# A delta-rule and feed-forward kernel: the first pair of chunks with another order, other queues and fewer norm steps

## Chip, cores and metric

One core of one Trainium2 chip. The metric is the device time of one execution in microseconds (us). The engines are PE (TensorE's products; PEld is its weight load), VectorE (DVE), ScalarE (ACT), GpSimd (POOL) and SyncE (SP). Transfers are issued by the queues of SP, ACT and POOL.

## The reference, cut to what matters

```python
# q, k, v: (4, 8, 768, 48), beta: (4, 8, 768), w_in: (384, 2048), w_out: (2048, 384)
k_n = k / (np.linalg.norm(k, axis=-1, keepdims=True) + 1e-06)
for t in range(S):
    y[:, :, t] = np.einsum('bhd,bhde->bhe', q[:, :, t], state)
    v_old = np.einsum('bhde,bhd->bhe', state, kt)
    state = state + bt[:, :, :, None] * np.einsum('bhd,bhe->bhde', kt, vt - v_old)
x = y.transpose(0, 2, 1, 3).reshape(B * S, H * D)
h = x @ w_in
g = np.where(h >= 1, h, np.where(h <= -1, 0.0, (h + 1) ** 2 / 4))
return g @ w_out
```

A recurrence over 768 steps for each of 32 heads, and behind it two matrix products with a clipped square between them, in float32. The two weight matrices come as 64-bit floats and are converted on the chip.

## The kernel before

The 768 steps are cut into 12 chunks of 64, and two chunks make a pair, so there are six pairs. For a chunk, the recurrence is turned into products: a gram matrix of the keys (gram_k, L229) and of keys and queries (gram_q, L242), the inverse of a unit triangular matrix for each head, and a chain of four products with the running state: chain_r, chain_u, chain_y, chain_d (L434 to L571). The inverse is made in three steps. Its diagonal blocks of 16 are solved on VectorE for a pair at once, with the 128 lanes as heads and blocks (lanes, L289; solve, L333: 15 steps of two operations; unlanes, L366, which scales the result and transposes it back into the tile XT). PE then merges blocks of 16 into 32 (merge16_a, merge16_b) and of 32 into 64 (merge32), each with a copy on ScalarE or VectorE behind it. In lanes, norms (L267) makes the norms of the keys from the diagonal of the gram matrix: a root on ScalarE and a step that sharpens it on VectorE.

The feed-forward part works on a pair's 512 token columns, for 16 tiles of 128 hidden units: up (L670) is nine products into one tile h, three operations of ScalarE and one of VectorE make s, a cast on ScalarE (ghi, L790) and a subtraction on VectorE (glo, L791) split it into a high and a low part, and down (L679) adds 12 products to the output's sums. For the first pair the first six tiles are run for the first chunk alone and later again for the second, so that this part can start as soon as chunk 0 is done.

Each weight tile f is 768 KB and is unpacked in five steps: grow (ScalarE, L187), shift and join (VectorE, L193 and L199), cast (ScalarE, L203), low (VectorE, L206). Up for tile f needs all five.

Every engine runs its list in order. The order around the first pair is written by hand. K, Q, KV and weight loads are issued at the start by load_k, load_q, load_kv and weight_loads; then PE runs the grams, 25 filling products on zeros (L629, two passes each in the trace), the merges and the chain of chunk 0. Between a stage's products and the copies that empty them, the letters of FRONT are run, and in the items of the feed-forward part those of FILL: A and D are the next weight step on ScalarE and VectorE, w and W the next weight load through SP or ACT, l the next other load, L a piece of lanes for the second pair of chunks, s, t, v and z half of scaling the values of chunk 0 to 3, m and M a mask of the queries, S a solve step, U a piece of unlanes, B a copy back. PIECES says in which half item PE runs which stage of chunks 1 to 3. The queues of the loads reuse eight semaphores in turn, so a load waits for the eighth before it.

At the end store_last (L703) copies the four output tiles and sends each in two halves.

## Time and profile before

| what | value |
|---|---|
| runs shown | median 610.14 us, 609.32 to 612.75 (3 runs) |
| the profiled execution | 611.8 us, of which the span of the core's instructions is 610.1 |
| mean granted clock of PE | 0.948 of full speed |
| busy share of the span | PE 95%, PEld 83%, DVE 65%, ACT 64%, POOL 5% |
| bytes moved | 42.77 MB, mean 70 GB/s |
| weight transfers | 16 of 768 KB, 14 from SP and 2 from ACT, median 5.7 and 5.4 us to landing |

The page cuts the span into 40 slices of 15.25 us and gives the busy share of each in tenths. A table of stretches gives the same for windows that one chooses. A timeline gives each instruction's start and duration, how long its engine stood idle before it, and what ended that. Busy time of PE is modelled from its pipelined products, so a full PE need not be at its peak; the granted clock says at what share of full speed it ran.

### The profile page before, as it was taken

The page shows a single profiled execution, that of the slowest core. Times are in us where ns is not written, and L with a number is a line of the kernel's source. Part 1 is how long each engine was busy: PE and PEld are TensorE (multiplying, and loading weights), DVE is VectorE, ACT ScalarE, POOL GpSimd, SP SyncE. Part 2 cuts the span into 40 slices and gives each one's busy share as a digit, 9 for nine tenths or more (in the row PEclk, how much of TensorE's full clock was granted, in tenths as well). Part 3 has the DMA queues.
Part 4 walks back from the last instruction along what each step waited for, and adds up shares of the span by engine and source line. Part 5 has one row for each costly group of instructions (what it writes and reads, how often), then busy time and mean ns, then how long its engine had stood idle before and what let it go on. Part 6 is the DMA issues. An engine that isn't in the chain of part 4 may idle for free.

```text
span 610.1 us, 21744 instructions
## 1 busy us (share of the span) xinstructions
PE 577.8 (95%) x9576; PEld 506.4 (83%) x9576; DVE 395.8 (65%) x835; ACT 393.2 (64%) x683; POOL 31.9 (5%) x63
## 2 busy tenths in 40 slices
PE   8847989799989999999999999999999999999996
PEld 7747978688978888888888888888888888889986
DVE  4977789982488963489954489954589944333332
ACT  3537688559756578646587647586746586666663
POOL 6110000010020000020000020000020000000000
PEclk8557599989999999999999999999999999999999
DMA  5672727210224110225110225111134000020001
GB/s 142 200 273 87 288 59 227 75 33 3 65 74 126 37 31 12 62 55 128 46 31 16 60 64 132 31 31 36 38 88 111 1 2 17 10 57 1 0 1 52
DMA packets 32542, 42.77 MB, mean 70 GB/s; under 512 B 7056, under 2 KB 27152, under 8 KB 32448
## 3 DMA queue, kind: packets, MB, share of 16 engines
q1 hardware_dynamic: 31072, 38.94, 22.1%
q10 hardware_dynamic: 1120, 2.36, 1.2%
q8 instruction: 75, 1.23, 0.9%
q14 instruction: 19, 0.16, 0.1%
q0 software_dynamic: 256, 0.08, 0.1%
HBM read 34.47 MB, written 4.72 MB: 64 GB/s over the span
## 4 chain that ended last, share of the span: by engine, by line
PE 68%; ACT 10%; SPq 6%; DVE 6%; DMA 6%; issue 2%; DVEq 0%; ACTq 0%
PE h L675 27%; PE o L690 27%; DMA wt<-in_w_dram 3%; PE ch L481 3%; ACT GG L429 2%; ACT s L795 2%; ACT XT L431 2%; PE ch L439 2%; PE ch L248 2%; PE ch L455 1%; PE ch L417 1%; PE ch L554 1%; PE ch L419 1%; ACT s L827 1%; DMA Q<-in_kqb_dram 1%
## 5 line engine op out<-in xcount | busy, mean ns | idle before, releaser
L675 PE MATMUL h<-xb,wt 128*128 128x512 f32 (+1 forms) x918 | 228.6, 393 | 4.6 <-DMA xb<-wt 2.3
L690 PE MATMUL o<-wt,ghi 128*128 128x384 f32 x768 | 200.7, 343 | 0.0
L675 PEld LDWEIGHTS h<-xb,wt 128*128 128x128 f32 x918 | 165.5, 193 | 38.8 <-issue 2.4
L829 DVE TENSOR_TENSOR s<-h,s 128x512 f32<-128x512 f32 (+1 forms) x102 | 66.7, 654 | 120.3 <-ACT s L827 120.0
L690 PEld LDWEIGHTS o<-wt,ghi 128*128 128x128 f32 x768 | 137.7, 189 | 7.1
L690 PE MATMUL o<-wt,glo 128*128 128x384 f32 x384 | 130.0, 339 | 1.9 <-DVE glo L791 1.9
L790 ACT CAST ghi<-s 128x512 fp32r<-128x512 f32 (+1 forms) x102 | 60.8, 596 | 102.0 <-DVE s L829 93.1
L795 ACT ACTIVATE s<-h,half 128x512 f32<-128x512 f32 (+1 forms) x102 | 67.6, 663 | 38.9 <-PE h L675 38.1
L791 DVE TENSOR_TENSOR glo<-s,ghi 128x512 fp32r<-128x512 f32 (+1 forms) x102 | 66.6, 653 | 38.7 <-ACT ghi L790 38.7
L690 PEld LDWEIGHTS o<-wt,glo 128*128 128x128 f32 x384 | 72.4, 189 | 2.8 <-DVE glo L791 2.8
L795 ACT ACTIVATE s<-s,one 128x512 f32<-128x512 f32 (+1 forms) x102 | 71.7, 702 | 2.3
L827 ACT ACTIVATE s<-s 128x512 f32<-128x512 f32 (+1 forms) x102 | 61.9, 607 | 3.2
L350 DVE TENSOR_TENSOR pr<-A 128x30 f32<-128x30 f32 (+14 forms) x120 | 39.3, 328 | 6.4 <-POOL A L321 4.5
L352 DVE TENSOR_TENSOR A<-A,pr 128x30 f32<-128x30 f32 (+14 forms) x120 | 39.9, 332 | 4.4
L481 PEld LDWEIGHTS ch<-Q,SU 64*64 64x64 f32 (+3 forms) x1056 | 22.5, 135 | 4.5 <-ACT ghi L790 1.5
L481 PE MATMUL ch<-Q,SU 64*64 64x64 f32 (+3 forms) x1056 | 24.7, 222 | 0.7 <-ACT SU L464 0.7
L262 DVE TENSOR_TENSOR Q<-ch,mask 64x512 f32<-64x512 f32 (+1 forms) x30 | 20.6, 687 | 0.9 <-PE ch L248 0.4
L321 POOL TENSOR_SCALAR_AFFINE_SELECT A<-A 128x1024 f32<-128x1024 f32 x4 | 5.1, 1265 | 301.3 <-DMA xb<-X 257.1
L187 ACT ACTIVATE xb<-wt 128x768 f32<-128x768 f32 x16 | 14.5, 905 | 8.9 <-DMA KV<-in_kv_dram 4.7
L417 PEld LDWEIGHTS ch<-XT,GG 32*32 32x32 f32 x768 | 14.9, 113 | 6.3 <-issue 4.2
L417 PE MATMUL ch<-XT,GG 32*32 32x32 f32 x768 | 16.4, 200 | 2.7 <-issue 1.0
L429 ACT ACTIVATE GG<-ch 32x512 f32<-32x512 f32 x24 | 14.1, 589 | 6.5 <-PE ch L417 6.2
(151 smaller groups left out, 595.1 us busy)
## 6 DMA issues: line engine op xcount, KB each, us to landing
wt<-in_w_dram SPq DMA_DIRECT2D x14, 768.0 KB, 5.7
out_dram<-wx SPq DMA_DIRECT2D x44, 96.0 KB, 2.2
KV<-in_kv_dram SPq DMA_DIRECT2D x36, 96.0 KB, 2.4
KV<-in_kv_dram SPq DMA_DIRECT2D x72, 48.0 KB, 2.3
KV<-in_kv_dram SPq DMA_DIRECT2D x12, 192.0 KB, 2.7
xb<-X SPq DMA_DIRECT2D x60, 32.0 KB, 2.0
K<-in_kqb_dram SPq DMA_DIRECT2D x12, 128.0 KB, 2.7
Q<-in_kqb_dram SPq DMA_DIRECT2D x12, 128.0 KB, 2.7
```

The costliest lines, as they stand in the source:

```text
L350: nc.vector.tensor_tensor(out=pr, in0=A[:, 0:n, j:j + 1].broadcast_to([P, n, m]), in1=A[:, j:j + 1, j + 1:32].broadcast_to([P, n, m]), op= ...
L352: nc.vector.tensor_tensor(out=A[:, 0:n, j + 1:32], in0=A[:, 0:n, j + 1:32], in1=pr, op=ALU.add)
L417: nc.tensor.matmul(y1[r:r + 32, u], GG[r + 32:r + 64, ga, u, 0:32], XT[r + 32:r + 64, ga, u, 32:64], start=True, stop=True)
L429: nc.scalar.mul(out=GG[r:r + 32, ga, :, 0:32], in_=y1[r:r + 32], mul=-1.0)
L481: nc.tensor.matmul(yy[i][o * C:o * C + C, e, p], SF[rows, u:u + C], w_[rows, x, k, :], **how)
L675: nc.tensor.matmul(h[:, cols(bs)], WT[f][:, 0, x, k * P:(k + 1) * P], XB[G][:, y, k, cols(bs)], start=(n == 0), stop=(n == 8))
L690: nc.tensor.matmul(oacc[G, k], (ghi, glo)[x][:, k * P:(k + 1) * P], WT[f][:, 1, y, :], start=(new and n == 0), stop=(left[G, b] == 0 and n ...
L790: nc.scalar.copy(out=ghi[:, c], in_=s[:, c])
L791: nc.vector.tensor_tensor(out=glo[:, c], in0=s[:, c], in1=ghi[:, c], op=ALU.subtract)
L795: nc.scalar.activation(out=out, in_=in_, func=AF.Relu, bias=bias, scale=scale)
L827: nc.scalar.activation(out=s[:, c], in_=s[:, c], func=AF.Square)
L829: nc.vector.tensor_tensor(out=s[:, c], in0=h[:, c], in1=s[:, c], op=ALU.max)
```

## The change

In the first lines of the program:
- load_k(1) issues four of its six loads from POOL instead of ACT;
- weight tiles 2, 3 and 4 are issued by SP ahead of load_kv(1), instead of tiles 2 and 3 behind it; ACT no longer issues weights;
- nine warm-up products of PE instead of 14.

In the first pair's work:
- norms reads the diagonal of the gram matrix in place, adds 1e-30 inside the root by a bias, and writes where the result is needed: one copy and one maximum on VectorE go;
- the copies of chunk 1 in lanes(0) are made in halves, four instead of two;
- the transpose of the norms is placed later;
- unlanes scales and transposes half s = 1 first, then half s = 0, instead of both at once;
- FRONT, FILL and PIECES have other values.

In store_last the copies of tiles 2 and 3 change engines, and each tile's second half is sent by ACT, POOL, POOL and ACT, where ACT sent all four.

```diff
-WARM = 14
+WARM = 9
 FRONT = (
-    "AL,L", ",WA", "sL,Amm", "DDmsD,", ",WAADw", "t,", "AtDDD,A")
+    "wsAALLsL,", "D,", "DD,", ",mm", "mt,AtA", "Dw,", "DADA,")
 FILL = (
-    "DD,,D,,w,AA", "ADA,D,D,DA,,B", ...
+    ",D,D,,,DAD", "ADD,Dw,ABADA,,DM,wlA", ...
-PIECES = ((0, "a1"), (1, "r1"), (2, "b1"), (4, "c1"), ... (8, "y1"), (11, "d1"), (16, "q2"), ...
+PIECES = ((1, "a1 r1"), (3, "b1"), (4, "c1"), ... (8, "y1"), (10, "d1"), (17, "q2"), ...
...
-    load_k(1, (nc.sync, nc.scalar))
+    load_k(1, (nc.sync, nc.gpsimd))
...
     load_kv(0)
+    weight_loads(2, 5)
     load_kv(1)
-    weight_loads(2, 4)
...
-    def norms(n):
-        y = sb.tile([P, 32], F32, name="y0")[:, 0:n.shape[1]]
-        r = sb.tile([P, 32], F32, name="r1")[:, 0:n.shape[1]]
-        nc.scalar.activation(out=y, in_=n, func=AF.Sqrt)
-        nc.vector.tensor_scalar(out=r, in0=y, scalar1=1e-30, scalar2=None, op0=ALU.max)
-        nc.vector.reciprocal(out=r, in_=r)
+    def norms(n, out):
+        y = sb.tile([P, 32], F32, name="y0")
+        r = sb.tile([P, 32], F32, name="r1")
+        nc.scalar.activation(out=y, in_=n, func=AF.Sqrt, bias=tiny)
+        nc.vector.reciprocal(out=r, in_=y)
...
-            for r in (0, C):
-                (nc.scalar.copy if G else nc.vector.tensor_copy)(out=x[r:r + 32, :, 32:64], in_=x[r:r + 32, :, 0:32])
+            for u in (half(0), half(1)) if (G, g) == (0, 1) else (slice(0, NU),):
+                for r in (0, C):
+                    (nc.scalar.copy if G else nc.vector.tensor_copy)(out=x[r:r + 32, u, 32:64], in_=x[r:r + 32, u, 0:32])
...
-        nc.vector.tensor_copy(out=n, in_=A.rearrange("l j t -> l (j t)")[:, 0:1024:33])
-        r = norms(n)
-        N = S["N", G] = sb.tile([P, 32], F32, name="N3")
-        nc.vector.transpose(out=N, in_=n)
+        r = norms(A.rearrange("l j t -> l (j t)")[:, 0:1024:33], n)
...
+        N = S["N", G] = sb.tile([P, 32], F32, name="N3")
+        if G:
+            nc.vector.transpose(out=N, in_=n)
...
-        for s in range(2):
+        for s in (1, 0):
             b = slice(16 * s, 16 * s + 16)
             nc.vector.tensor_tensor(out=X32[:, b, b], in0=X[:, s], in1=gm[:, None, b].broadcast_to([P, 16, 16]), op=ALU.mult)
-        yield
-        if G:
-            nc.gpsimd.memset(ZT[:, :, :, 16:32], 0.0)
-        nc.vector.transpose(out=XT[:, :, :, 32:64].rearrange("p g u t -> p t (g u)"), in_=X32.rearrange("l c t -> l t c"))
-        yield
+            if G and s:
+                nc.gpsimd.memset(ZT[:, :, :, 16:32], 0.0)
+            nc.vector.transpose(out=XT[:, :, :, 32 + 16 * s:48 + 16 * s].rearrange("p g u t -> p t (g u)"), in_=X32[:, :, b].rearrange("l c t -> l t c"))
+            yield
...
     def store_last(G):
         o = [sb.tile([P, 2, DM], F32, name="wx", bufs=2) for _ in range(2)]
-        for k in range(TT + 1):
-            if k < TT:
-                (nc.scalar.copy, nc.vector.tensor_copy)[k % 2](out=o[k // 2][:, k % 2], in_=oacc[G, k])
-                send(G, k, 0, o[k // 2], nc.sync)
-            for x in ((0,), (), (1,), (), (2, 3))[k]:
-                send(G, x, 1, o[x // 2], nc.scalar)
+        for k in range(TT):
+            x = o[k // 2][:, k % 2]
+            (nc.scalar.copy if k in (0, 3) else nc.vector.tensor_copy)(out=x, in_=oacc[G, k])
+            send(G, k, 0, o[k // 2], nc.sync)
+            send(G, k, 1, o[k // 2], (nc.scalar, nc.gpsimd, nc.gpsimd, nc.scalar)[k])
```

ScalarE's list before, from the copy of beta to the first cast (wt0 to wt5 are weight tiles, xb the tile in which they are unpacked, y0 the root of the norms, XT and GG the triangular blocks, SU the state):

```order
L154 COPY beta_sb_80<-o0_525 128x160
L187 ACTIVATE xb_182<-wt0_110 128x768
L393 COPY wt12_142<-o1_528 128x256
L271 ACTIVATE y0_603<-N2_601 128x32
L122 DMA wt4_684<-in_w_dram 128x1536
L187 ACTIVATE xb_182<-wt1_112 128x768
L429 ACTIVATE GG_176<-ch_687 32x16x32 x2
L187 ACTIVATE xb_182<-wt2_136 128x768
L424 COPY XT_177<-h_735 32x16x32 x2
L464 COPY SU_175<-o2_776 64x384 x2
L122 DMA wt5_815<-in_w_dram 128x1536
L203 CAST wt0_817<-xb_182 128x2x384
```

The same place now:

```order
L154 COPY beta_sb_80<-o0_525 128x160
L188 ACTIVATE xb_181<-wt0_110 128x768
L188 ACTIVATE xb_181<-wt1_112 128x768
L272 ACTIVATE y0_605<-A_598,tiny_170 128x32
L395 COPY wt12_144<-o1_528 128x256
L431 ACTIVATE GG_175<-ch_693 32x16x32 x2
L426 COPY XT_176<-h_734 32x16x32 x2
L466 COPY SU_174<-o2_772 64x384 x2
L188 ACTIVATE xb_181<-wt2_125 128x768
L204 CAST wt0_815<-xb_181 128x2x384
```

The grow steps of tiles 0 and 1 and the root stand ahead of the copy after merge16_a (L393, now L395); the grow step of tile 2 has moved from ahead of the copy after merge32 (L424, now L426) to behind the copies of the state.

SyncE's list before, at the end of the loads of chunk 1's keys and values (KV_125):

```order
L115 DMA KV_125<-in_kv_dram 128x192
L117 DMA KV_125<-in_kv_dram 64x192 x2
L122 DMA wt2_136<-in_w_dram 128x1536
L122 DMA wt3_138<-in_w_dram 128x1536
L122 DMA wt6_821<-in_w_dram 128x1536
L122 DMA wt7_1007<-in_w_dram 128x1536
L91 DMA K_1196<-in_kqb_dram 64x512
```

Now, at the start of those loads (KV_131; KV_114 is chunk 0's):

```order
L117 DMA KV_114<-in_kv_dram 64x192 x2
L122 DMA wt2_125<-in_w_dram 128x1536
L122 DMA wt3_127<-in_w_dram 128x1536
L122 DMA wt4_129<-in_w_dram 128x1536
L111 DMA KV_131<-in_kv_dram 64x384
```

Tiles 2 to 4 have moved ahead of chunk 1's nine loads; tiles 5 to 8 follow these.

VectorE's list before, in the norms of the second pair of chunks (gm is beta over the squared norm, A16 the blocks to be solved, ch in L405 the product of merge16_b):

```order
L276 TENSOR_SCALAR N2_601<-r1_604 128x32
L313 STREAM_TRANSPOSE N3_611<-N2_601 128x32
L315 RECIPROCAL r1_604<-N2_601 128x32
L316 TENSOR_TENSOR gm_613<-r1_604,beta_sb_80 128x32
L317 TENSOR_TENSOR gm_613<-gm_613,r1_604 128x32
L405 TENSOR_TENSOR XT_177<-XT_177,ch_617 128x16x16
L406 STREAM_TRANSPOSE GG_176<-XT_177 128x16x32
L283 TENSOR_TENSOR KV_114<-KV_114,N3_441 128x384
L328 TENSOR_TENSOR A16_721<-A_594,gm_613 128x256 x2
```

Now:

```order
L276 TENSOR_SCALAR N2_604<-r1_606 128x32
L313 RECIPROCAL r1_606<-N2_604 128x32
L314 TENSOR_TENSOR gm_612<-r1_606,beta_sb_80 128x32
L315 TENSOR_TENSOR gm_612<-gm_612,r1_606 128x32
L318 STREAM_TRANSPOSE N3_616<-N2_604 128x32
L283 TENSOR_TENSOR KV_114<-KV_114,N3_444 128x384
L329 TENSOR_TENSOR A16_619<-A_598,gm_612 128x256 x2
L194 TENSOR_SCALAR xb_181<-xb_181 128x768
L407 TENSOR_TENSOR XT_176<-XT_176,ch_625 128x16x16
L408 STREAM_TRANSPOSE GG_175<-XT_176 128x16x32
```

The step behind merge16_b (L405, now L407) has moved behind the scaling of a value tile (L283), the blocks A16 and a shift of weight tile 0 (L194).

More of the change, by code (lines that the diff above doesn't have):

```diff
@@ L29 @@
 FRONT = (
-    "AL,L", ",WA", "sL,Amm", "DDmsD,", ",WAADw", "t,", "AtDDD,A")
+    "wsAALLsL,", "D,", "DD,", ",mm", "mt,AtA", "Dw,", "DADA,")
 FILL = (
-    "DD,,D,,w,AA", "ADA,D,D,DA,,B", ",,,lD,,ww", "ADMw,DD,D,wAMAD,wDBMS,A", ",D,,D,,S", ",AD,DAw,D,D,w", "lDS,AS,A,D,lAD,", ",AD,,,DD,SAD",
-    "S,ADA,,Sw,,", ",SD,S,DASvD,S,SS", "vAS,DASll,,,UU,D", "A,ADDDD,,DUAD,,", ",DAD,,,,D", ",,,,zl,", ",,,,,", "D,,,,z,")
+    ",D,D,,,DAD", "ADD,Dw,ABADA,,DM,wlA", ",AD,Sw,D,A,", "DM,,ADD,,DAM,l", ",DB,wwD,,,D", ",S,DwASA,,w,wD", "ADSD,A,D,,S,wAS", ",DA,,DD,AlD,SD",
+    "A,S,AD,,D,S", ",,D,AS,,SvS", "lADS,,vSDA,SU,D,", "DD,DAU,A,DUlD,,", "A,,D,D,,", "A,,,,,", ",,,lDD,,", "D,,,,,", ",,,,,z", "z,,,,,")
 MERGE = 28
-PIECES = ((0, "a1"), (1, "r1"), (2, "b1"), (4, "c1"), (5, "e1"), (6, "u1"), (8, "y1"), (11, "d1"), (16, "q2"), (19, "r2"), (23, "a2"), (24, "a3"), (25, "b2"), (27, "b3 q3"))
+PIECES = ((1, "a1 r1"), (3, "b1"), (4, "c1"), (5, "e1"), (6, "u1"), (8, "y1"), (10, "d1"), (17, "q2"), (20, "r2"), (23, "a2"), (24, "a3"), (25, "b2"), (26, "b3"), (27, "q3"))
 @with_exitstack
@@ L170, in delta_rule_moe @@
     nc.vector.memset(one, 1.0)
-    root = const.tile([P, 1], F32, name="root")
-    nc.scalar.activation(out=root, in_=mid, func=AF.Sqrt)
+    tiny = const.tile([P, 1], F32, name="tiny")
+    nc.vector.memset(tiny, 1e-30)
+    nc.scalar.activation(out=sb.tile([P, 32], F32, name="y0")[:, 0:1], in_=mid, func=AF.Sqrt, bias=tiny)
     SF = const.tile([P, 2 * NU * D + C - D], F32, name="SU")
@@ L265, in gram_q @@
         return evict
-    def norms(n):
-        y = sb.tile([P, 32], F32, name="y0")[:, 0:n.shape[1]]
-        r = sb.tile([P, 32], F32, name="r1")[:, 0:n.shape[1]]
-        nc.scalar.activation(out=y, in_=n, func=AF.Sqrt)
-        nc.vector.tensor_scalar(out=r, in0=y, scalar1=1e-30, scalar2=None, op0=ALU.max)
-        nc.vector.reciprocal(out=r, in_=r)
+    def norms(n, out):
[3 more added lines that the diff above has]
+        nc.vector.reciprocal(out=r, in_=y)
         nc.vector.tensor_tensor(out=r, in0=r, in1=n, op=ALU.mult)
         nc.vector.tensor_tensor(out=r, in0=r, in1=y, op=ALU.add)
-        nc.vector.tensor_scalar(out=n, in0=r, scalar1=0.5, scalar2=1e-6, op0=ALU.mult, op1=ALU.add)
+        nc.vector.tensor_scalar(out=out, in0=r, scalar1=0.5, scalar2=1e-6, op0=ALU.mult, op1=ALU.add)
         return r
@@ L328, in lanes @@
             nc.vector.tensor_tensor(out=A16[:, s], in0=A[:, b, b], in1=gm[:, b, None].broadcast_to([P, 16, 16]), op=ALU.mult)
+        if G == 0:
+            nc.vector.transpose(out=N, in_=n)
         X32 = S["X32"] = sb.tile([P, 32, 32], F32, name="A", bufs=1)
@@ L607, in delta_rule_moe @@
     loads = [(load_k, 3), (load_q, 2), (load_kv, 2), (load_q, 3), (load_kv, 3), (load_k, 4)]
-    tile_ = [4]
+    tile_ = [5]
     def do(codes):
@@ L646, in delta_rule_moe @@
     stage(one_(merge32, 0, None, True), 2)
-    stage(one_(merge32, None, 0), 3)
+    stage(one_(merge32, None, 0, True), 3)
     stage(both(chain_u, 0), 4)
```

## The prediction, made before the result was known

> **What bounds the kernel now.** I read the page first (busy shares and slices), then a table of stretches, then the waits of the first 130 us, then the timeline of each engine there. The page's span and its row of granted clock:
>
> ```profile
> span 610.1 us, 21744 instructions
> PE 577.8 (95%) x9576; PEld 506.4 (83%) x9576; DVE 395.8 (65%) x835; ACT 393.2 (64%) x683; POOL 31.9 (5%) x63
> PEclk8557599989999999999999999999999999999999
> ```
>
> PE is busy nearly everywhere, so time can be won only where it waits or runs at a lower clock: the first fifth, which is the part that the change rewrites. The table of stretches (us; busy time of PE, PEld, DVE, ACT and POOL; granted clock; DMA):
>
> ```profile
> 40.00:50.00 10.00, 4.80 (x114) 4.16 (x112) 4.56 (x10) 4.38 (x7) 0.00 (x0) 0.50 0.83 318
> 60.00:70.00 10.00, 10.00 (x228) 9.36 (x225) 6.63 (x13) 6.92 (x13) 1.04 (x2) 0.50 0.71 249
> 70.00:80.00 10.00, 10.00 (x211) 9.02 (x213) 7.52 (x13) 8.15 (x16) 0.53 (x1) 0.71 0.47 193
> 90.00:100.00 10.00, 10.00 (x109) 8.84 (x108) 9.64 (x20) 9.43 (x14) 0.00 (x0) 1.00 0.69 230
> 110.00:120.00 10.00, 7.11 (x154) 5.59 (x154) 9.79 (x20) 4.82 (x8) 0.00 (x0) 1.00 0.34 93
> ```
>
> Three limits follow each other: from 40 to 50 no engine is even half busy, so all wait for a transfer or for each other; from 60 to 80 PE is full, at half clock most of the time; from 90 on VectorE is full and PE waits for it. The waits of the first 130 us (us in total, times, longest):
>
> ```profile
> PE o L455 <- ACT XT L424: 4.5, 1, 4.5
> PE h L675 <- DMA xb<-wt: 2.3, 3, 1.7
> PE o L690 <- DVE glo L791: 1.5, 1, 1.5
> ```
>
> The largest is one chain: PE's chain_u(0) (L455) waits for ScalarE's copy L424, which stands in ScalarE's queue behind a weight step (L187) that waits for its weight tile. ScalarE's timeline there (start, duration, idle before):
>
> ```profile
> 29.09 0.29 ACT L154 COPY beta_sb<-o 128x160 f32<-128x160 f32 x1 [1.67 <-PE o L151]
> 29.28 0.92 ACT L187 ACTIVATE xb<-wt 128x768 f32<-128x768 f32 x1
> 30.95 0.37 ACT L393 COPY wt<-o 128x256 f32<-128x256 f32 x1 [0.76 <-PE o L386]
> 31.36 0.23 ACT L271 ACTIVATE y<-N 128x32 f32<-128x32 f32 x1
> 42.79 0.89 ACT L187 ACTIVATE xb<-wt 128x768 f32<-128x768 f32 x1 [4.23 <-DMA wt<-in_w_dram]
> 43.71 1.18 ACT L424 COPY XT<-h 32x512 f32<-32x512 f32 x2
> ```
>
> **The block on ScalarE.** Its cause stands in the queue of SyncE, which sends weight tiles 2, 3, 6 and 7 only here:
>
> ```profile
> 35.67 3.06 SPq L122 DMA_DIRECT2D wt<-in_w_dram  x4
> 44.98 0.34 PE L455 MATMUL o<-KV,XT 64*64 64x48 f32 x2 [4.46 <-ACT XT L424]
> ```
>
> PE was done with the products that L424 copies at 44.98 - 4.46 = 40.52. The change sends tiles 2 to 4 ahead of the nine transfers of KV(1), by this row's 0.77 each some 7 us sooner, and puts the step for tile 2 behind L424 and L464 in ScalarE's order. L424 then starts at about 40.55, ends 1.18 later, and PE starts at about 41.8: **-3.2 us**, if what lies ahead keeps its time. What is late next is PE itself. KV(1) now leaves SyncE 3 x 0.77 = 2.3 later; its first reader stands in VectorE's order behind the masks, which before were two thirds done at 38.91 (row L193, below), so that is covered; uncovered it would cost up to 2.3. The two weight transfers that ScalarE itself issued go to SyncE's queue; nothing waited for these issues.
>
> **What lies ahead.** VectorE gets there sooner: the copies of the second chunk in halves, norms without one copy and one maximum, and the transpose of the solved blocks in two parts. Rows of PE and VectorE:
>
> ```profile
> 22.68 5.54 PE L629 MATMUL o<-SU 128*64 128x32 f32 x50
> 28.98 1.91 PE L386 MATMUL o<-XT,GG 32*32 32x16 f32 x128
> 35.57 1.75 PE L417 MATMUL ch<-XT,GG 32*32 32x32 f32 x58 [0.98 <-issue]
> 25.13 0.76 DVE L371 TENSOR_TENSOR A<-X,gm 128x256 f32<-128x256 f32 x2
> 25.93 2.21 DVE L375 STREAM_TRANSPOSE XT<-A 128x1024 f32<-128x1024 f32 x1
> 28.04 1.00 DVE L377 STREAM_TRANSPOSE XT<-A 128x512 f32<-128x512 f32 x1
> 31.62 0.18 DVE L272 TENSOR_SCALAR r<-y 128x32 f32<-128x32 f32 x1 [0.30 <-ACT y L271]
> 31.84 0.35 DVE L273 RECIPROCAL r<-r 128x32 f32<-128x32 f32 x1
> 33.71 0.41 DVE L405 TENSOR_TENSOR XT<-XT,ch 128x256 f32<-128x256 f32 x1
> ```
>
> PE's first merge (L386) needs only the later half of XT. Before, that came 0.76 + 2.21 = 3.0 us after the solve; now it comes after half of L371 and a transpose of 512 elements, 0.38 + about 1.0 (the L377 row) = 1.4, so 1.6 us sooner; the norms lose a maximum (31.62 to 31.84) and a copy of about that length, 0.4. With a little from the halves VectorE gains 2.0 or more. But PE runs its 50 filling products from 22.68 to 28.22, and the change leaves their number. XT was ready at 28.14, no later than they ended. **VectorE's lead is spent waiting behind them: 0 us.** Were these products at double speed, 5.54 / 2 = 2.8 of it would come through; that is the far bound.
>
> The next two places move the other way. ScalarE now has two weight steps and the root ahead of the copy L393: 29.28 + 2 x 0.92 + 0.23 = 31.35, so the copy ends at about 31.75 instead of 31.32. VectorE then runs the rest of the norms, 33.71 - 31.84 = 1.87, and behind them three things that used to stand after L405 (the fourth row belongs to the end of the front):
>
> ```profile
> 34.79 0.52 DVE L283 TENSOR_TENSOR KV<-KV,N 128x384 f32<-128x384 f32 x1
> 35.23 0.75 DVE L328 TENSOR_TENSOR A<-A,gm 128x256 f32<-128x256 f32 x2
> 38.91 0.56 DVE L193 TENSOR_SCALAR xb<-xb 128x768 int32<-128x768 int32 x1
> 53.16 0.55 DVE L283 TENSOR_TENSOR KV<-KV,N 128x384 f32<-128x384 f32 x1
> ```
>
> From 31.38 that is 1.87 + 0.44 (34.79 to 35.23) + 0.7 + 0.5 = 3.5, so L405's successor starts at about 34.9, 1.2 later than at 33.71. PE had a gap of 0.98 just behind its first products there (the L417 row), in which nothing of the other engines held it; if it now falls into the wait, PE ends these products at 37.2 as before, otherwise 0.9 later. I take +0.3 (nearer to a hidden gap, since the gap has no releaser). At the end of the front the KV row at 53.16 no longer stands ahead of the low part of weight tile 0, for which PE waited: -0.5. **Front: -3.2 + 0.3 - 0.5 = -3.4**, between -2.3 (gap kept, no other gain) and -6.2 (filling products at double speed).
>
> **K through POOL, fewer warm-up products.** POOL issued beta's transfers at these rates (duration in ns; then us to landing):
>
> ```profile
> L633 POOL DMA_DIRECT2D beta_sb<-in_beta_dram x8: 524/534/739, 6.4 to 10.5; - x8
> DMA to landing us min/median/max: 2.3/2.8/3.8
> 8.26 0.68 PE L235 MATMUL h<-K 48*64 48x64 f32 x26 [0.56 <-DMA K<-in_kqa_dram]
> ```
>
> Four of them, now first in POOL's queue, take 2.1; from about 1 us on they land by 5.5 to 7, against a wait for K until 8.26. That is up to 2 gained for VectorE's chain, and nothing lost if these larger transfers take twice as long to issue; either way, and with the five warm-up products fewer, it ends in the cover of the filling products: 0 us (without that cover, the same up to 2 gained). POOL's own fills behind them move by 2 us, from about 6.4 to 8.5; their first reader, the solve, can't start before K's products, their copies, a transpose and the norms.
>
> **From 55 to 140 us.** The order of PE's stages hardly changes. On ScalarE one cast is gone from ahead of the copies of chain_y(1), whose six transfers PE awaits for 2.3 us:
>
> ```profile
> 79.91 0.82 ACT L203 CAST wt<-xb 128x768 fp32r<-128x768 f32 x1
> 83.92 3.97 SPq L542 DMA_DIRECT2D xb<-wt  x6
> ```
>
> I take -0.7 there, and -0.3 for VectorE's shorter work around the solve, where it is full: **-1.0**, between +1.5 (a second stall like L690's 1.5) and -4 (the 2.3 and the 1.5 of the waits gone). Tiles 12 to 15 are now queued behind those six transfers; they would leave at about 80, and their first reader is behind the item that itself waits for the six, so this is covered by some 2 us.
>
> **The last stores.** ScalarE's last three issues take 1.93 from 604.81, the last landing 2.2 to 2.6 after its issue:
>
> ```profile
> 604.04 2.40 SPq L701 DMA_DIRECT2D out_dram<-wx  x4
> 604.81 1.93 ACTq L701 DMA_DIRECT2D out_dram<-wx  x3
> DMA to landing us min/median/max: 2.2/2.4/2.6
> ```
>
> ScalarE's ended at 606.74 and SyncE's at 606.44; over three queues SyncE's is the last, 0.3 sooner. But by beta's rows POOL's transfer may land up to 1.2 later than these (3.8 against 2.6): **-0.2**, between -0.5 and +0.9.
>
> Sum: -3.4 - 1.0 - 0.2 = **-4.6 us**. The profiled execution took 611.8 in all (span 610.1), which gives 607.2. The median of the runs shown is 610.14, 1.7 below it, so I forecast 605.5 against the median.
>
> **The rivals.**
>
> *The clock comes up sooner.* From 60 to 80 PE had a clock of 0.50 and 0.71: 15.8 of 20 us at half speed (0.71 = 1 - 0.58 / 2). With the gap of 4.5 us ahead of it gone, PE may reach this stretch at full clock. PE would gain up to 7.9, but VectorE was busy 6.63 + 7.52 = 14.2 of these 20 us, so at most 5.8; I take 5: 600.5. For it: the clock changes within this stretch at the same work. Against it: 10 us of a full PE did not raise it, so it is not the gap alone. The Trainium skill ("TensorE: Matmul & The Clock Gate", Part 1) says that some 3.4 us of sustained activity release the throttle; by that rule the stretch would be at full clock from about 64 on. The row of 60 to 70 disagrees here, PE 10.00 busy at 0.50, so small products seem not to count fully. Chance 0.16.
>
> *The gain is given back where VectorE is full.* From 90 to 120 it is busy 9.6 to 9.8 of 10, and the new order puts the last weight's low part behind both merges. Two more stalls of PE like the 1.5 of L690 cost 3.0: 608.5, no change that a measurement shows. For it: the 110 to 120 row (PE 7.11, DVE 9.79). Against it: the work itself is not more. Chance 0.20.
>
> *Slower: the half clock lasts on.* It rises at about 76, within products of the first items. If the new hooks open a wait of PE just there, it stays at half into the stretch behind; each us at half costs 0.5 while PE is the bound. It decides the sign once 4.6 / 0.5 = 9 us more are at half; with 20 us more the time is 605.5 + 10 = 615.5. For it: nothing but the late rise. Against it: PE stayed at 1.00 from 110 to 120 with 2.9 us of gaps. Chance 0.08.
>
> *The change does less than it says* is in the forecast already, as VectorE's lead that ends behind the filling products.
>
> **How the numbers follow.** My forecast has 0.56, its own range 603 to 607. About 0.5% (3.05 us, so 607.1) is what a measurement of this kernel can tell from no change. Faster: 0.56 + 0.16 = 0.72; same 0.20; slower 0.08. The range leaves out the slower rival and the lower half of the clock's: 601.0 to 609.5.
>
> **What would show it.** Right: no wait of the successor of L424 for a weight step, PE's chain_u(0) at 41 to 43, PE's first merge still at 28 to 29 behind the filling products though XT is ready by 26, the successor of L405 at about 35, the low part of weight tile 0, which followed the row at 53.16, started 3 to 4 us sooner than 53.7. Wrong: a first merge at 25 to 26 (the lead came through), a wait of ScalarE for weights somewhere else, a half clock of a length other than some 16 us behind 55, or waits of PE for VectorE between 80 and 130 that add up to more than before.

## The result, and the profile after

The changed kernel took 606.92 us (median of 7) against 610.68 us for the kernel before (7), a ratio of 0.9943 with a 95% interval of 0.992 to 0.9967: 3.5 us faster. A second series (9 and 26 executions) gave 607.42 against 611.09, ratio 0.9933 (0.9909 to 0.9958). The forecast was 605.5. The total is close to it; the places that it came from are not. The traced execution of the first series, and the only traced one of e5 below, ran at a mean granted clock of 0.736 and 0.555 instead of about 0.95; the ratios leave such executions out, and the trace shown of the changed kernel is from the second series (606.55 us, span 604.8). Its lines of code stand one to three lower than before's (L455 is now L457, L386 is L388, L690 is L692).

From the page of the changed kernel, its span, PE's share and the row of granted clock:

```profile
span 604.8 us, 21718 instructions
PE 576.3 (95%) x9566; PEld 504.9 (83%) x9566; DVE 395.3 (65%) x828; ACT 393.2 (65%) x683; POOL 35.1 (6%) x69
PEclk9557599999999999999999999999999999999999
```

PE's busy time is 1.5 us less (577.8 before), so most of the gain is waits that are gone. Where, shows the start of the same steps in both traces (us; glo is a VectorE step that runs once per item of the feed-forward part, so it marks the progress of the items):

```text
step                        before    changed   difference
chain_u(0) on PE             44.98      44.65      -0.33
glo of item 0                61.83      61.97      +0.14
glo of item 5                91.20      90.65      -0.55
glo of item 12              129.67     128.32      -1.35
glo of item 14              146.88     142.91      -3.97
glo of item 19              174.95     170.20      -4.75
glo of item 101 (the last)  602.31     597.02      -5.29
span                        610.08     604.84      -5.24
```

(Before's traced execution was 0.7 above the median of the second series and the changed kernel's 0.9 below, so 1.6 of these 5.2 us are chance of these two executions.) The front, where the prediction put -3.4, gives nothing in this pair of traces. Almost all comes between items 5 and 19. The table of stretches of the changed kernel, whose row of 110 to 120 answers to the one shown of before (PE 7.11 there):

```profile
110.00:120.00 10.00, 8.24 (x271) 6.53 (x272) 9.72 (x18) 4.94 (x8) 0.00 (x0) 1.00 0.23 67
130.00:140.00 10.00, 10.00 (x285) 8.58 (x286) 4.97 (x8) 6.49 (x12) 0.00 (x0) 1.00 0.02 4
```

The second row for the kernel before:

```profile
130.00:140.00 10.00, 9.20 (x275) 7.63 (x274) 5.19 (x9) 3.96 (x7) 1.03 (x2) 0.83 0.02 6
```

In the kernel before, PE's clock fell to half for 3.4 us at 133.7 (a mean of 0.83 over these ten us); in the changed one it didn't. That is 1.7 us. It is not settled by the order alone: e7, e9 and e10 below have the changed order and the same two waits of PE at 110 to 120 us, and their traces show 3.4 us at half clock from 114 to 116 on, while those of e1 and e11 show none. The longest waits of the changed kernel from 55 to 141 us (us in total, times, longest):

```profile
PE ch L441 <- issue: 1.6, 1, 1.6
PE h L677 <- DMA xb<-wt: 1.5, 3, 0.9
PE ch L388 <- DVE KV L447: 1.0, 1, 1.0
PE h L677 <- DVE s L830: 0.7, 1, 0.7
```

Of the kernel before there, besides the 2.3 for xb and the 1.5 for glo that the prediction shows:

```profile
PE h L675 <- DVE wt L206: 1.2, 2, 0.9
PE ch L386 <- DVE XT L375: 1.1, 1, 1.1
PE ch L248 <- DVE XT L405: 0.8, 1, 0.8
```

The waits for xb fell from 2.3 to 1.5, as predicted (-0.7). The 1.5 for glo ahead of L690 and the 1.1 for XT ahead of L386 have become 1.0 for KV and 0.7 for s, and of the 1.2 and the 0.8 nothing is left.

**The front.** PE's timeline of the changed kernel (start, duration, idle before; before's rows stand in the prediction):

```profile
27.09 1.91 PE L388 MATMUL o<-XT,GG 32*32 32x16 f32 x128
31.80 1.91 PE L402 MATMUL ch<-wt,XT 32*32 32x16 f32 x128 [2.81 <-ACT wt L395]
35.46 0.64 PE L419 MATMUL ch<-XT,GG 32*32 32x32 f32 x16 [1.75 <-DVE XT L407]
38.65 1.49 PE L419 MATMUL ch<-XT,GG 32*32 32x32 f32 x48 [2.55 <-issue]
44.65 0.34 PE L457 MATMUL o<-KV,XT 64*64 64x48 f32 x2 [1.31 <-issue]
```

And ScalarE's there:

```profile
27.38 1.72 ACT L188 ACTIVATE xb<-wt 128x768 f32<-128x768 f32 x2
31.09 0.35 ACT L272 ACTIVATE y<-A,tiny 128x32 f32<-128x32 f32 x1 [2.00 <-DVE A L308]
31.35 0.35 ACT L395 COPY wt<-o 128x256 f32<-128x256 f32 x1
43.38 1.18 ACT L426 COPY XT<-h 32x512 f32<-32x512 f32 x2 [2.00 <-PE h L421]
```

Several steps come when predicted: the copy L395 ends at 31.70 (31.75 predicted), the correction L407 starts at 34.99 (34.9), and L426, L424's successor, waits for PE and no longer for a weight step. The first agreement is luck: the prediction had ScalarE busy up to there with two weight steps and the root, but the weight steps ended at 29.10, and the root then waited 2.00 us for VectorE. But inside L419, after 16 of 64 products, PE stands still for 2.55 us with nothing of the other engines to wait for, where 0.98 stood before. The 1.31 at L457, which the profile calls "issue" too, is the time of L426's copy. So ScalarE's block went, and a gap of PE took its place.

### The profile page after: what moved, and what is told of

Its sections match the earlier page's. It is cut to its first block, busy times and chain, and to the rows that moved or that the text cites. A ratio compares the mean times of both kernels' runs of the same rounds, so it can differ in the third digit from the quotient of the medians.

```text
span 687.5 us, 21718 instructions
## 1 busy us (share of the span) xinstructions
PE 666.7 (97%) x9566; PEld 548.0 (80%) x9566; DVE 396.9 (58%) x828; ACT 397.7 (58%) x683; POOL 35.1 (5%) x69
## 3 DMA queue, kind: packets, MB, share of 16 engines
q8 instruction: 75, 1.23, 0.7%
## 4 chain that ended last, share of the span: by engine, by line
PE 64%; issue 29%; DVE 4%; DMA 1%; ACT 1%; POOL 1%; SPq 0%; ACTq 0%; POOLq 0%; DVEq 0%
PE h L677 24%; PE o L692 23%; PE ch L483 3%; PE ch L419 2%; PE ch L441 2%; PE ch L236 2%; PE ch L249 1%; PE ch L556 1%; PE ch L457 1%; PE ch L421 1%; DMA K<-in_kqa_dram 1%; DVE X L344 1%; DVE pr L342 1%; DVE A L308 1%; PE ch L388 1%
## 5 line engine op out<-in xcount | busy, mean ns | idle before, releaser
L677 PE MATMUL h<-xb,wt 128*128 128x512 f32 (+1 forms) x918 | 267.6, 444 | 0.5 <-DMA xb<-wt 0.3
L692 PE MATMUL o<-wt,ghi 128*128 128x384 f32 x768 | 232.5, 389 | 0.0
L677 PEld LDWEIGHTS h<-xb,wt 128*128 128x128 f32 x918 | 174.7, 203 | 56.7 <-DMA xb<-wt 1.5
L692 PEld LDWEIGHTS o<-wt,ghi 128*128 128x128 f32 x768 | 149.6, 201 | 21.7
L692 PE MATMUL o<-wt,glo 128*128 128x384 f32 x384 | 148.6, 387 | 0.0
L692 PEld LDWEIGHTS o<-wt,glo 128*128 128x128 f32 x384 | 76.4, 199 | 5.7
L483 PEld LDWEIGHTS ch<-Q,SU 64*64 64x64 f32 (+3 forms) x1056 | 26.2, 155 | 4.7 <-issue 3.1
L483 PE MATMUL ch<-Q,SU 64*64 64x64 f32 (+3 forms) x1056 | 28.7, 242 | 0.0
L419 PEld LDWEIGHTS ch<-XT,GG 32*32 32x32 f32 x768 | 15.6, 118 | 8.6 <-issue 6.8
L419 PE MATMUL ch<-XT,GG 32*32 32x32 f32 x768 | 17.1, 204 | 4.1 <-issue 2.5
L466 ACT COPY SU<-ch 64x384 f32<-64x384 f32 (+1 forms) x30 | 14.3, 476 | 6.9 <-PE ch L457 6.5
```

The lines of the kernel that those rows point to most:

```text
L419: nc.tensor.matmul(y1[r:r + 32, u], GG[r + 32:r + 64, ga, u, 0:32], XT[r + 32:r + 64, ga, u, 32:64], start=True, stop=True)
L483: nc.tensor.matmul(yy[i][o * C:o * C + C, e, p], SF[rows, u:u + C], w_[rows, x, k, :], **how)
L677: nc.tensor.matmul(h[:, cols(bs)], WT[f][:, 0, x, k * P:(k + 1) * P], XB[G][:, y, k, cols(bs)], start=(n == 0), stop=(n == 8))
L692: nc.tensor.matmul(oacc[G, k], (ghi, glo)[x][:, k * P:(k + 1) * P], WT[f][:, 1, y, :], start=(new and n == 0), stop=(left[G, b] == 0 and n ...
```

## The experiments

**Which queue place of the weights.** The changed kernel again (e0_after), and three edits: the changed kernel with the weight transfers back behind KV(1)'s, the kernel before with its weights ahead of KV(1)'s, and the kernel before with the new last stores.

```diff
-    weight_loads(2, 5)
     load_kv(1)
+    weight_loads(2, 5)
```

e0_after, the changed kernel itself:

> The changed kernel once more, for a trace of it at an undisturbed clock. Theory A (the front gained what the prediction says): the chain_u(0) products of PE start at 41 to 43 us and the first up product at about 50. Theory B (the front's gain is eaten by gaps of PE that nothing of the other engines explains, 2.6 and 2.5 us ahead of merge products, and the measured 3.7 us come from behind 55 us): chain_u(0) at about 44.6, first up product at 53, and from 55 to 140 us PE waits, or runs at half clock, 3 us less than before.

Measured: 607.42 us, chain_u(0) at 44.65, the first up product at 53.64 (53.13 before). Theory B on the front; behind 55 us PE waits and runs at half clock less, as shown above.

e1_weights_late, the diff above on the changed kernel:

> The changed kernel with the transfers of weight tiles 2 to 4 put back behind KV(1)'s in SyncE's queue; nothing else. Theory A (the sooner weights are what takes ScalarE's wait away): the weight step waits again at about 43, wherever ScalarE's order now has it, and the time is level with the changed kernel or up to 3 us longer. Theory B (the sooner weights fill the DMA engines at 31 to 39 us, and PE's own fetches of instructions come late by that): the two gaps of 2.6 and 2.5 us shrink to below 1 each, chain_u(0) starts 2 to 3 us sooner, at 41 to 42.5, and the time is 0 to 3 us shorter than the changed kernel's. Theory C (the gaps lie at fixed places of PE's program): gaps of 2.6 and 2.5 as in the changed kernel.

Measured: 606.12 us, ratio to before 0.9904 (0.9866 to 0.9941), not told apart from the changed kernel's 0.9933. PE's timeline:

```profile
35.46 0.64 PE L419 MATMUL ch<-XT,GG 32*32 32x32 f32 x16 [1.66 <-DVE XT L407]
36.39 1.49 PE L419 MATMUL ch<-XT,GG 32*32 32x32 f32 x48 [0.29 <-issue]
42.40 0.34 PE L457 MATMUL o<-KV,XT 64*64 64x48 f32 x2 [1.31 <-issue]
```

The same products start at the same 35.46, after the same 16 of them stands the gap, and it is 0.29 instead of 2.55 us. Nothing of PE's program differs; only transfers of other data were moved. That is theory B for this gap, against C. The other gap that theory B named, ahead of L402, was not one: the undisturbed trace puts it down to the copy L395, and it stayed (3.04). ScalarE did not wait for the late weights either, against A: the new order of its weight steps alone removes the block, and their sooner transfer was not needed.

e2_before_weights_soon, the reverse move on the kernel before:

```diff
+    weight_loads(2, 4)
     load_kv(1)
-    weight_loads(2, 4)
```

> The kernel before with only the transfers of weight tiles 2 and 3 moved ahead of KV(1)'s. Theory A (ScalarE's wait for weights is the price): L424's copy starts at about 40.6 instead of 43.7, chain_u(0) at about 42, and the time falls by some 3 us. Theory B (a fuller DMA at 31 to 39 us delays PE's fetches): the wait for weights is gone as well, but PE's gaps ahead of L400 and L417 grow by 1 to 2 us each, chain_u(0) starts at 43 to 45, and the time falls by 0 to 1.5 us.

Measured: 611.27 us, ratio 1.0013 (0.9989 to 1.0036), no change. PE's timeline:

```profile
33.31 1.84 PE L400 MATMUL ch<-wt,XT 32*32 32x16 f32 x122 [1.92 <-issue]
37.58 1.75 PE L417 MATMUL ch<-XT,GG 32*32 32x32 f32 x58 [1.49 <-issue]
43.85 0.34 PE L455 MATMUL o<-KV,XT 64*64 64x48 f32 x2 [1.31 <-ACT XT L424]
```

Theory B again: ScalarE's block is gone (PE's wait of 4.46 is 1.31), but the gaps of 0.54 and 0.98 grew to 1.92 and 1.49, and chain_u(0) came only 1.1 us sooner than in the trace of the kernel before.

e3_before_tail, the new last stores alone:

```diff
-        for k in range(TT + 1):
-            if k < TT:
...
+            send(G, k, 1, o[k // 2], (nc.scalar, nc.gpsimd, nc.gpsimd, nc.scalar)[k])
```

> The kernel before with only the last stores of the change (their queues and copies). The prediction's term: 0.2 us shorter, between 0.5 shorter and 0.9 longer. If the tail were where the change's 3.7 us come from, 2 us or more shorter; if GpSimd's transfer lands late, 0.5 to 1 longer.

Measured: 610.24 us, ratio 0.9988 (0.9966 to 1.001): not told apart from none. From the start of SyncE's last four issues to the end of the span it is 6.04 us before (604.04 to 610.08), 5.91 here (599.87 to 605.78) and 6.09 in the changed kernel (598.75 to 604.84). The term of -0.2 is -0.13 here and +0.05 in the changed kernel.

This trace shows one thing more, since up to the last stores its program is that of the kernel before. ScalarE's and PE's rows:

```profile
39.57 0.91 ACT L187 ACTIVATE xb<-wt 128x768 f32<-128x768 f32 x1 [0.73 <-DMA wt<-in_w_dram]
40.85 1.18 ACT L424 COPY XT<-h 32x512 f32<-32x512 f32 x2 [0.36 <-PE h L419]
42.12 0.34 PE L455 MATMUL o<-KV,XT 64*64 64x48 f32 x2 [1.31 <-ACT XT L424]
```

Here the weight step waits 0.73 us and not 4.23, the copy behind it waits for PE, and chain_u(0) starts at 42.12, without any of the new front: 2.86 sooner than in the trace of the kernel before and 2.53 sooner than in that of the changed kernel. So the block of 4.46 us that the prediction prices is not in every execution of the kernel before; how often it is there, these traces don't tell. The lead was kept: glo of item 0 starts at 59.09 and the last one at 598.14, 2.74 and 4.17 sooner than before.

**Order or shorter steps.** Four kernels for what acts behind 55 us, and for the front without its gap.

e4_order_old: the changed kernel with FILL and PIECES of before (its first entry gets one A and one D more, which the new front leaves undone):

```diff
-FILL = (",D,D,,,DAD", "ADD,Dw,ABADA,,DM,wlA", ...
+FILL = ("ADDD,,D,,w,AA", "ADA,D,D,DA,,B", ...
-PIECES = ((1, "a1 r1"), (3, "b1"), ...
+PIECES = ((0, "a1"), (1, "r1"), (2, "b1"), ...
```

> The changed kernel with the hooks behind 55 us (the tables FILL and PIECES) as before; the front, VectorE's shorter steps, the queues and the stores stay changed. Theory O (the new order behind 55 us is where the 3.7 us come from): PE's waits ahead of L692 and L388 at 110 to 120 us are back (2.5 us together), and so is the 3.4 us stretch at half clock at about 134; 2.5 to 4 us longer than the changed kernel, about 610. Theory W (it is VectorE's shorter steps and the sooner transfers that make the room, whatever the order): within 1 us of the changed kernel.

Measured: 611.0 us, ratio 1.0012 (0.9991 to 1.0032; 0.9933 with the new order): all of the gain is gone. PE's timeline:

```profile
113.34 0.44 PE L692 MATMUL o<-wt,glo 128*128 128x384 f32 x1 [1.52 <-DVE glo L792]
117.06 0.73 PE L677 MATMUL h<-xb,wt 128*128 128x512 f32 x2 [0.53 <-DVE s L830]
118.80 2.90 PE L677 MATMUL h<-xb,wt 128*128 128x512 f32 x7 [1.00 <-DVE wt L207]
```

The wait for glo is back. The merge itself, at 115.28, no longer waits, but the up products behind it now wait 0.53 for s and 1.00 for weights. A stretch of 3.4 us at half clock is there again too, at 119 instead of 134.

e5_order_new: the kernel before with the changed FILL and PIECES, the reverse replacement (without the first A and D of FILL).

> The kernel before with only the hooks behind 55 us of the change (its FILL, less the one A and one D that the old front has already done, and its PIECES). Theory O (the order is the gain): 2.5 to 4 us shorter than before, about 607, without the wait of 1.5 ahead of L690 and without the half clock at 134. Theory W (the shorter steps make the room): 1 us shorter at most, and the waits of PE at 110 to 120 stay above 2 us.

Measured: 614.26 us (613.99 without the execution that the ratio leaves out), ratio 1.0053 (1.0027 to 1.008). Both theories fall: the new order without the new steps is 3 to 4 us slower than before (by the ratio and by the medians), so neither half of the change gains behind 55 us by itself. Where it loses them no trace here shows.

e6_old_steps: the changed kernel with the norms and the transposition of before.

```diff
-        r = norms(A.rearrange("l j t -> l (j t)")[:, 0:1024:33], n)
+        nc.vector.tensor_copy(out=n, in_=A.rearrange("l j t -> l (j t)")[:, 0:1024:33])
+        r = norms(n)
...
-        for s in (1, 0):
+        for s in range(2):
...
+        nc.vector.transpose(out=XT[:, :, :, 32:64].rearrange("p g u t -> p t (g u)"), in_=X32.rearrange("l c t -> l t c"))
+        yield
```

> The changed kernel with the norms and the transposition of the solved blocks in the steps of before (one copy and one maximum more, one transposition of 1024 instead of two of 512); the order stays. From the changed kernel's trace the later half of XT comes 26.4 us, and by the old steps 1.6 later, at 28.0. Theory A (the split brings the first merge forward): the first merge at about 28.9 instead of 27.3, L407 about 0.4 to 1.6 later, and 0.3 to 1.5 us longer in all. Theory C (PE's start behind the filling products and its fetches decide): the time of the changed kernel within 0.5 us.

Measured: 614.52 us, ratio 1.0069 (1.0047 to 1.0091), 7 to 8 us above the changed kernel and far outside both theories. The first merge was at 28.26. Little of the loss is in the front (glo of item 0 at 62.58, 0.6 behind the changed kernel's): PE's merge of the second pair stood still for 6.55 us, which neither theory had priced:

```profile
120.57 1.90 PE L391 MATMUL ch<-XT,GG 32*32 32x16 f32 x128 [6.55 <-DVE XT L380]
```

e8_split_first was made for that: the split kept for the first pair and undone for the second alone.

```diff
+        if G:
+            for s in range(2):
+                b = slice(16 * s, 16 * s + 16)
+                nc.vector.tensor_tensor(out=X32[:, b, b], in0=X[:, s], in1=gm[:, None, b].broadcast_to([P, 16, 16]), op=ALU.mult)
+            yield
+            nc.gpsimd.memset(ZT[:, :, :, 16:32], 0.0)
+            nc.vector.transpose(out=XT[:, :, :, 32:64].rearrange("p g u t -> p t (g u)"), in_=X32.rearrange("l c t -> l t c"))
+            yield
-        for s in (1, 0):
+        for s in () if G else (1, 0):
```

> The changed kernel with the split of the solved blocks' transposition kept for the first pair and undone for the second (its multiplications in one step, its transposition whole in the next). Theory S (the second pair's split, together with the hooks that are laid out for it, is what the change gains from): PE's merge at about 114 (L388) waits some 6 us for the whole transposition, as it waited 6.55 with all old steps, and the time is 5 to 7.5 us longer than the changed kernel's, 612 to 615. Theory R (the norms or the first pair's split carried the loss that the old steps showed): at most 2 us longer than the changed kernel, and PE's wait there stays near 1.

Measured: 613.43 us, ratio 1.0033 (1.0016 to 1.0049), theory S. PE's merge, and the stretch around it (granted clock 0.52):

```profile
119.55 1.91 PE L396 MATMUL ch<-XT,GG 32*32 32x16 f32 x128 [6.56 <-DVE XT L378]
```

```profile
117.00:124.00 7.00, 4.45 (x134) 3.96 (x135) 6.32 (x8) 3.06 (x5) 0.00 (x0) 0.52 0.11 31
```

What the split does there is read from VectorE's timeline, first of the kernel before:

```profile
113.27 0.68 DVE L791 TENSOR_TENSOR glo<-s,ghi 128x512 fp32r<-128x512 f32 x1
113.87 0.76 DVE L371 TENSOR_TENSOR A<-X,gm 128x256 f32<-128x256 f32 x2
114.66 2.27 DVE L375 STREAM_TRANSPOSE XT<-A 128x1024 f32<-128x1024 f32 x1
```

And of the changed kernel:

```profile
109.77 0.68 DVE L792 TENSOR_TENSOR glo<-s,ghi 128x512 fp32r<-128x512 f32 x1
112.71 1.23 DVE L377 STREAM_TRANSPOSE XT<-A 128x512 f32<-128x512 f32 x1
113.83 0.97 DVE L447 TENSOR_TENSOR KV<-KV,ch 128x384 f32<-128x384 f32 x2
118.52 0.42 DVE L374 TENSOR_TENSOR A<-X,gm 128x256 f32<-128x256 f32 x1
118.98 1.21 DVE L377 STREAM_TRANSPOSE XT<-A 128x512 f32<-128x512 f32 x1
```

Before, both halves had to be through (0.76 + 2.27) before the merge could start. Now the merge starts behind the half that it needs, 112.71 + 1.23, and KV's step; the other half (0.42 + 1.21) follows at 118.52. The new order counts on that: it puts the merge between the two. With whole transpositions the merge waits for the later place (6.56), and with the old order the two halves stand together and nothing is won in all (e4). Split and order are one edit here.

What the split is worth apart from the places isn't shown. In e8 the whole transposition, 2.22 us long, starts only at 117.18, 4.65 behind the end of its multiplications, because the new order has its second place there. A whole step at the first place was not tried. Worked out from the rows above it would let the merge start at about 112.25 + 0.76 + 2.22 + half of KV's 0.97 = 115.7, an estimate, 1.3 us behind the 114.40 of the changed kernel. So most of e8's wait is a step that stands in the wrong place.

**The front once more.** e7_norms_behind: late weights as in e1, and the norms of the second chunk behind the correction L407.

```diff
-    "wsAALLsL,", "D,", "DD,", ",mm", "mt,AtA", "Dw,", "DADA,")
+    "wsAAL,", "s,LL", "DDD,", ",mm", "mt,AtA", "Dw,", "DADA,")
```

> The changed kernel with the transfers of weight tiles 2 to 4 behind KV(1) and, besides, the second chunk's norms behind the first correction L407 instead of ahead of it, so that ScalarE's copy L395 no longer stands behind the root and L407 no longer behind the norms. PE's wait of 3.04 ahead of L402 and of 1.66 ahead of L419 should go: L402 at about 29.4, L419 at about 32.1, chain_u(0) at 39 to 39.5 instead of 42.4. Theory F (what the front gains reaches the end): about 3 us shorter than with the weights alone put back, 603. Theory K (PE's clock returns to full at a time that the front does not move, 75 to 77 us, and what PE does sooner it does at half clock): at most half of it is left, 604.5 to 606, and the stretch at half clock becomes longer by about the lead.

Measured: 605.23 us, ratio 0.9915 (0.9884 to 0.9945). PE's timeline:

```profile
32.50 0.64 PE L419 MATMUL ch<-XT,GG 32*32 32x32 f32 x16 [0.56 <-DVE XT L407]
34.26 1.49 PE L419 MATMUL ch<-XT,GG 32*32 32x32 f32 x48 [1.12 <-issue]
40.26 0.34 PE L457 MATMUL o<-KV,XT 64*64 64x48 f32 x2 [1.31 <-issue]
```

chain_u(0) is 4.39 sooner than in the changed kernel; glo of item 0 is 2.35 sooner (59.62 against 61.97), and the ratios differ by 0.0018, 1.1 us, with intervals that overlap. The stretch at half clock that ends ahead of item 3 is 20.5 us long instead of 17.1, and the stretch at full clock in front of it 3.4 instead of 6.8. This is K's size, half of the lead or less, but K's reason only in part: the return to full clock did move, from 77.3 to 73.7. What did not change is the sum at half clock up to item 3: 58.0 (rounded, 41.0 and 17.1) in the kernel before and the changed one, 58.0 (37.5 and 20.5) in e1 and e7. (Later, e7 has 3.4 us more at half, from 114.6, behind waits of 0.95 and 0.67; the changed kernel had the same waits and no such stretch.) The clock is also not all that took of the lead: between chain_u(0) and item 0, e7 has two gaps of PE without a releaser, 2.05 us at 53.35 and 0.76 at 56.80, and the changed kernel one of 1.55 at 58.72.

e10_norms_weights_soon is e7 with the weights where the change has them.

> The changed kernel with the second chunk's norms behind L407, and the weight transfers where the change has them, ahead of KV(1)'s. Theory B (the sooner weights hold up PE's fetches): gaps of PE that nothing explains come back ahead of or within L402 and L419, 3 to 5 us together instead of 1.5 with late weights, each ending 1.2 to 1.5 us after a late packet of the instruction queue has landed; chain_u(0) at 42 to 44 instead of 40.3; 0.5 to 1.5 us longer than with late weights. Theory C (the gaps belong to PE's program): 1.5 us of gaps, chain_u(0) at 40.3, the same time.

Measured: 606.44 us, ratio 0.992 (0.9897 to 0.9943). Theory B:

```profile
32.64 0.64 PE L419 MATMUL ch<-XT,GG 32*32 32x32 f32 x16 [0.56 <-DVE XT L407]
37.68 1.49 PE L419 MATMUL ch<-XT,GG 32*32 32x32 f32 x48 [4.40 <-issue]
43.68 0.34 PE L457 MATMUL o<-KV,XT 64*64 64x48 f32 x2 [1.31 <-issue]
```

The gap after the same 16 products is 4.40 against 1.12, and chain_u(0) comes 3.4 us later than in e7. In the time it doesn't show: the ratios, 0.992 and 0.9915, are not told apart. The stretch of 34 to 38 us of e10, then of e1 (DMA share in the last column but one; it adds up the packets' times over 16 engines and can pass 1):

```profile
34.00:38.00 4.00, 0.32 (x13) 0.32 (x14) 3.81 (x11) 0.00 (x0) 1.86 (x3) 0.50 1.03 363
```

```profile
34.00:38.00 4.00, 2.13 (x64) 1.91 (x64) 3.94 (x9) 0.08 (x1) 2.27 (x3) 0.50 0.63 187
```

In the same stretch the share is 0.49 in e7 and 1.03 in the changed kernel. The page lists 75 packets of queue q8, "instruction", with 1.23 MB, 16 KB each. Among the DMA records the last of them ahead of each gap (us):

```text
kernel, line      packet starts   landed    PE goes on   behind it   gap
before, L417          32.85        34.10        35.57        1.47      0.98
e2,     L400          31.09        32.05        33.31        1.26      1.92
e2,     L417          34.99        36.24        37.58        1.34      1.49
changed, L419         36.14        37.17        38.65        1.48      2.55
e1,     L419          34.09        35.02        36.39        1.37      0.29
e4,     L419          35.53        36.50        37.91        1.41      1.82
e7,     L419          31.90        32.96        34.26        1.30      1.12
e10,    L419          35.23        36.22        37.68        1.46      4.40
```

In all eight PE goes on 1.3 to 1.5 us after the packet has landed, whatever the length of the gap. (The same place has gaps of 2.47, 2.29 and 2.43 us in e6, e8 and e11, which end 1.59, 1.45 and 1.6 us behind their packet.) With weights in the rings the packet starts 3.3 us later (e10 against e7) or 2.0 (changed against e1).

e9_few_fill is e7 with 3 instead of 25 filling products (IDLE).

> The kernel with late weights and norms behind (605.23 us; its own filling products at 20.6 to 26.1 us) with 3 filling matmuls instead of 25, so 5 us of PE's idle time in their place. Theory N (they only cover; XT's later half is ready at 26.4, so the first merge comes at most 0.5 us sooner): the time within 0.6 us. Theory G (PE's work there raises the granted clock later): the stretches at half clock up to 80 us become longer by 3.4 or more, and the time by 1.5 us or more.

Measured: 604.95 us, ratio 0.9895 (0.9871 to 0.9919), theory N. The first merge now waits for the half of XT that it needs:

```profile
26.56 1.91 PE L388 MATMUL o<-XT,GG 32*32 32x16 f32 x128 [3.68 <-DVE XT L377]
```

It is 0.46 us sooner than e7's (27.02), and the sum at half clock stays 58.0. It is the fastest version tried; the next kernel, nearly the changed one and in the same series, took 606.93. The intervals of the two still overlap (up to 0.9919, and from 0.9911).

e11_k_scalar: the changed kernel with K(1)'s second transfers and the warm-up products of before.

```diff
-    load_k(1, (nc.sync, nc.gpsimd))
+    load_k(1, (nc.sync, nc.scalar))
-WARM = 9
+WARM = 14
```

> The changed kernel with K(1)'s second transfers in ScalarE's queue again and 14 warm-up products: the prediction's term of 0. Expected: the first merge within 1 us of 27.3, the time within 0.6 us of the changed kernel. Rival (the sooner K starts everything sooner): the solve's start and the first merge 1 to 1.7 us later, and 0.8 to 1.7 us longer.

Measured: 606.93 us, ratio 0.9937 (0.9911 to 0.9964), the first merge at 27.67. The term of 0 holds.

## Why the prediction was right in the total and wrong in the places

The total came out by luck. The -3.4 of the front did not come, the -1.0 behind 55 us was some 2.5 us too small, and the two errors nearly cancel.

- **ScalarE's block, -3.2.** The mechanism was right (no wait for weights is left at L426) and the condition failed that it was put under: "if what lies ahead keeps its time". The weights sent sooner filled the DMA engines just where PE needed its next 16 KB of instructions, and PE's gap grew from 0.98 to 2.55. The prediction asked what queues the transfers were moved past and found KV(1)'s 2.3 covered; it did not ask who else uses the DMA engines. Of all the steps this is the one that failed. Its price, besides, was read from one execution: in e3's trace, with before's front, the weight step waits 0.73 us and PE 1.31, so there the 3.2 was not to be won at all.
- **+0.3 for the gap "nearer to a hidden gap".** The reason given, that it had no releaser, was wrong: the releaser is a packet that the waits don't name. Without the sooner weights (e1) chain_u(0) comes at 42.40, 0.6 behind the 41.8 that the prediction started from, so the other terms of the front were well sized: 0.3 of the 0.6 was in it.
- **Each us of the front at a full us.** Not settled. From 12 to 50 and on to 77 us PE runs mostly at half clock, and that sum was 58 us in both kernels and in e1, e7 and e9 alike. If that sum were given, an idle us removed there would be filled with work at half clock and worth half a us later. The leads over the changed kernel at chain_u(0) did shrink: 2.25 became 1.29 by item 0 in e1, and 4.39 became 2.35 in e7; 4.66 in e9 was still 4.13 at item 0, but 1.2 at the end of the span. But gaps of PE without a releaser are longer there, by 0.8 in e1 (2.34 against 1.55 ahead of L441) and by 1.3 in e7, and e9 lost 1.7 in its stretch of 3.4 us at half clock at 114. And the sum is not given: it goes in steps of 3.41 us (17 of them make 58.0), about as long as the leads, and in e3, with the same front as before, it is two steps less, 51.2, and there the lead of 2.86 was kept. By the ratios of the times 1.1 us of e7's lead and 2.3 of e9's are left, with intervals that overlap the changed kernel's.
- **The filling products.** "VectorE's lead is spent waiting behind them" failed as said, since they moved too: PE ended K's products sooner and they ran from 20.79 to 26.33, so the first merge came at 27.09 and not at 28 to 29. Its 1.9 us were then lost at L402, behind the root in ScalarE's queue, which waited for VectorE. The 0 of that line came out right for another reason.
- **-0.5 for the low part of weight tile 0.** It started at 53.10, not 3 to 4 sooner than 53.7, because chain_u(0) was late. PE's wait of 0.95 for it is gone all the same, and the first up products end at 55.20 instead of 55.74. By the glo of item 0 nothing is left of that.
- **55 to 140 us, -1.0.** Wrong in size, and in what it rests on. The -0.7 for xb held (2.3 to 1.5). The -0.3 for "VectorE's shorter work around the solve" was the place where the change gains most: the split was priced for the first pair alone, where nothing came of it, and not for the second, whose merge stands where VectorE is full. By e4 (4.8 us by the ratios, 1.0012 against 0.9933) and e8 (6.1 us, 1.0033 against 0.9933) that split with the order around it carries the whole measured gain; neither tells the two shares apart. The prediction's bound of -4 for this stage took it in.
- **The rivals.** The gain given back where VectorE is full did not happen; the opposite did. Of "the clock comes up sooner" one part came: not the long stretch, which is as long as before (17.1 us), but the short one at 134 is gone, in this pair of traces. "Half clock lasts on" did not come, yet e8 shows that such a thing exists: 4.2 us into its wait of 6.56 us the clock fell, and it stayed at half for 6.8 us.
- **K, warm-up, stores.** 0, 0 and -0.2 against 0 for both by e11 (0.9937, and 0.9933 with the change) and between -0.13 and +0.05 for the stores.

What stays open: why the sum at half clock up to item 3 is 58 us in the traces of eight of these kernels, 54.6 in those of e2, e4 and e10, and 51.2 in that of e3, whose front is before's (the mean granted clock of the 72 executions of the kernel before in the three series lies between 0.944 and 0.966, so it differs between executions of one program); what the split is worth without the order; and whether the packets come late because their DMA engines work off the weights first. The runs show that moving the weights moves the packet and the gap, not by what rule the engines choose.

## What to carry to other kernels

A transfer that is sent sooner can delay others that use the DMA engines at that time, here the instruction fetch of PE: look at the DMA share of the stretch that it lands in, and put it where that share is low or the engine idles anyway (34 to 38 us had 0.63 without and 1.03 with it). A step split in two can free its reader where the engine that runs it is full and the reader needs one half, but here only with the order rewritten for it; test such edits together and apart, since here each alone was neutral or slower. Read a stall from more than one trace before pricing it: the largest wait of the kernel before, 4.46 us, was 1.31 in another execution of the same front. And do not expect a lead to arrive whole: of leads of 4.4 and 4.7 us over the changed kernel at chain_u(0), 1.1 and 1.2 were left at the last item of the traces, after other gaps of PE and another stretch at half clock.
